# Attention with a spectral mix: in the full runs the value sums leave their PSUM bank after every run, and that bank also holds score tiles; scores and maxima over 64 rows

## The chip, the cores and the metric

The kernel runs on one core of a Trainium2 chip. The metric is the device time of one execution in microseconds (us). All matmuls are fp32 data: most are in the one-pass form (tiles of type F32R, split by the kernel into a high and a low part), the value products of the attention in the plain fp32 form.

## The reference

The kernel computes a gated mix of two layers over a sequence of 2048 rows of 512.

```python
g = _sigmoid((x * gate_w).sum(-1, keepdims=True))
a = _A_ref(x, dft_seq_re, dft_seq_im, dft_hid_re, dft_hid_im)   # y = Cr @ (x Hr^T) - Ci @ (x Hi^T)
b = _B_ref(x, wqkv, wo)                                          # softmax attention, 32 heads of 16
return g * a + (1 - g) * b
```

For each head the attention needs scores `q @ k^T / 4` (2048 x 2048), a softmax over them, and the product with the values (16 columns). The softmax here takes off each row's maximum, so the scores are worked out twice: once for the maxima, once for the exponentials.

## The kernel before

**Stages.** First come the projections of q and k, then those of v together with one half of the hidden transform, then a long middle part that runs the attention of all heads and, beside it, the sequence transform, and last the output projection. Heads are handled in pairs (`p`, 16 of them). A pair's q and k stand in `qs[p % 2]` and `ks[p % 2]`: head `h` of the pair has partitions 64h to 64h+47 (16 rows each of high times high, high times low, low times high). Rows 64h+48 and 64h+49 of `qs` take the negated row maxima (high and low part), the same rows of `ks` are ones, so that the scores come out of the matmul with the maximum already taken off. `load_stacks` loads a pair, `m_parts` and `m_rows` make the rows of maxima: VectorE reduces and transposes, GpSimd splits, and eight small DMAs write the rows, four of them issued by GpSimd for head 1 and the rest by SyncE.

**Three kinds of matmul share the tensor engine.** `a_tile` computes a 128 x 512 tile `a` of raw scores over 48 rows, and VectorE takes its maxima (`mx`). `scores` computes a 128 x 512 tile `s` over 50 rows, and ScalarE writes its exponentials to `pt`. `d` is a chain of 48 products, each in two halves of 64 rows, that accumulates one 128 x 512 tile of the sequence transform (class `Chain`, `dft`); its end is copied out by ScalarE (`y`). A `d` on one half of the array's rows and an `a` or `s` on the other half run at the same time. The fourth kind are the value products in `pv`: for each unit (`u`, a pair's block of 128 keys against 1024 queries) four matmuls with 17 columns of weights (16 values and a column of ones) and all 128 rows, each on its own strip of 32 columns of the array, accumulating in `acc`.

**Runs.** The order on every engine is written out by hand. The middle part is a sequence of runs (`segment`), each one following a pattern of slots. A slot issues one `d` and one `a` or `s`; `|` issues the value products of one unit. There are 26 runs of the thin patterns, then 192 of the pattern `FULL` (96 pairs of runs, the two halves of the same `d` operands), then 26 of the pattern `NINE`. A full run has 16 `d`, 8 `s`, 8 `a` and two units of value products. The digit behind a slot's letter is the PSUM bank of its tile. The first `d` of a run waits for the reader of the tile that the last slot of the run before made, and the last value product of a full run waits, by a dependency added by hand, for the run's last exponential (`exponential`).

**PSUM.** There are eight banks of 128 x 512 fp32: six (`six`, numbers 0 to 5) turn over among `s` and `a` tiles, one holds the tile `d`, and one holds `acc`. The sums of a pair's half of the queries accumulate in `acc` over 16 units (8 runs); then `acc` is copied to `oe` in SBUF (by VectorE in full runs, by ScalarE elsewhere) and two DMAs store it.

**GpSimd's queue.** GpSimd splits the chunks of the sequence transform's matrix into high and low parts (`c_split`: a cast and a subtraction for every 12 operands of `d`, each chunk needing its loaded `craw` and a pair of buffers that the `d` matmuls have finished with), makes the parts of the maxima, issues its four row DMAs, and does some multiplications of the normalisation (`no`, `nh`). All of this stands in one queue, in program order.

Of the kernel before, what the change touches and what calls it, by code (L numbers as in the profile page):

```python
# [31 lines left out]
def mix_kernel(ctx: ExitStack, tc: tile.TileContext, xa_t, xa, wqkv, w_hid, w_seq, wo, gate_w, out):  # L32
# [8 lines left out]
    six = [ctx.enter_context(tc.tile_pool(name=f"ps{i}", bufs=1, space=PSUM)) for i in range(6)]  # L41

    used = list(range(6))

    class Ring:
# [5 lines left out]
        def tile(self, shape, dtype, name, bank=None):  # L51
            i = min(self.banks, key=used.index) if bank is None else bank
            t = six[i].tile(shape, dtype, name=name, tag="t")
            self.touch(i)
            self.of[id(t)] = (t, i)
            return t
# [11 lines left out]
    psO = ctx.enter_context(tc.tile_pool(name="psO", bufs=1, space=PSUM))  # L68
# [6 lines left out]
    qk_d = [dram.tile([2, D, S], F32, name=f"qk{c}") for c in range(2)]  # L75
    b_d = [dram.tile([P, 2, D], F32, name=f"b{s}") for s in range(NT)]
# [21 lines left out]
    acc = psO.tile([P, 512], F32, name="acc")  # L98
# [179 lines left out]
    def a_tile(i, h, ps=None, bank=None):  # L278
# [4 lines left out]
        r = slice(64 * h, 64 * h + 48)  # L283
# [34 lines left out]
    nc.gpsimd.memset(ones, 1.0)  # L318
    nc.gpsimd.memset(vt[:, :, :, 16:17], 1.0)
    load_stacks(0)  # L320
    wos = [staged(wo[:, kt]) for kt in range(KT)]
    for i in range(2):
        for h in range(2):
            for tb in range(2):
                nc.sync.dma_start(ks[i][64 * h + 48:64 * h + 50, tb * 2 * D:(tb + 1) * 2 * D].bitcast(F32), ones)
# [433 lines left out]
    pts = {}  # L759

    def scores(u, qb, h, bank=(psS, "s"), number=None):
# [11 lines left out]
        rr = slice(64 * h, 64 * h + 50)  # L773
# [14 lines left out]
    def pv(u, full=False):  # L788
# [4 lines left out]
        pt = pts.pop(u)  # L793
        for j in range(4):
            h = j % 2
            i = nc.tensor.matmul(acc[32 * j:32 * j + 17], vt[:, kt, p, 16 * h:16 * h + 17], pt[:, j],  # L796
                                 start=kt == 0, stop=kt == NT - 1)
        if kt == NT - 1:
            oe = work.tile([P, 512], F32, name="oe", bufs=2)
            if full:  # L800

                nc.vector.tensor_copy(oe, acc)
            else:
                nc.scalar.copy(oe, acc)
            for qb in range(2):
                nc.sync.dma_start(o_d[hf][p, :, qb * 512:(qb + 1) * 512], oe[64 * qb:64 * qb + 64])
# [70 lines left out]
    FULL = "s2 a3 s4 a1 s5 s2 a0 s3 a4 s1 a5 s2 a0 s3 a4 a1 | |"  # L877
# [10 lines left out]

    streams = [stream(h) for h in range(2)]
# [11 lines left out]
    def values(full=False):  # L901
        nonlocal valued
        i = pv(valued, full)
# [3 lines left out]
    def segment(pattern, half, ds, stop):  # L907
# [5 lines left out]
        for n, slot in enumerate(pattern.split()):  # L913
# [3 lines left out]
            if slot == "|":  # L917
                i = values(pattern == FULL)
# [129 lines left out]
```

## Time and profile before

| | |
|---|---|
| time, median of 3 runs | 1698.53 us (1698.32 to 1698.54) |
| span of the profiled execution | 1696.8 us |
| granted TensorE clock, mean | 0.999 |
| instructions | 33721 |
| VectorE busy | 81% |
| ScalarE busy | 67% |
| GpSimd busy | 26% |

The profile is of one execution. Its span reaches from the first to the last instruction; the time of a run is a little longer. TensorE counts as busy whenever a matmul is in flight, and matmuls are pipelined, so that a busy TensorE may still be held up. In the rows of the profile PE is TensorE's matmuls, PEld its weight loads, DVE is VectorE, ACT ScalarE, POOL GpSimd and SP SyncE; L774 is line 774 of the kernel before, and a tile stands under its name in the program (`acc`, `s`, `a`, `d`, `pt`).

### The profile page before, as it was taken

To read this page: it belongs to the slowest core of one execution; us is meant where nothing else is said; L and a number is where in the kernel's file an instruction comes from. 1 tells how busy PE (TensorE), PEld (TensorE's weight loads), DVE (VectorE), ACT (ScalarE), POOL (GpSimd) and SP (SyncE) were. 2 spreads that over 40 slices of the span, in tenths; PEclk is the share of its full clock that TensorE was granted. 3 is DMA by queue.
4 is the path that set the end of the run, shared out by engine and by line. 5 is a ranking of instruction groups with operands and counts; after the bars stand their busy time and mean duration, and the time that the engine had idled before them with its cause. 6 is when DMAs were issued, how large, how long until landed. Compare 5 with 4: busy or idle time off the path is not lost.

```text
span 1696.8 us, 33721 instructions
## 1 busy us (share of the span) xinstructions
PE 1689.2 (100%) x13040; PEld 1076.1 (63%) x13040; DVE 1366.7 (81%) x2313; ACT 1138.6 (67%) x2242; POOL 449.6 (26%) x554
## 2 busy tenths in 40 slices
PE   9999999999999999999999999999999999999998
PEld 7888855556666666666666666666666666655544
DVE  5439888888888888888888888888888888889854
ACT  5212377777766777666777677776667776678886
POOL 0101122322222333222222343322323343211110
PEclk9999999999999999999999999999999999999999
DMA  8963600314141434314156435224141535362114
GB/s 294 344 146 132 161 8 13 47 39 76 57 76 46 88 98 97 73 39 82 38 95 243 96 108 109 68 63 77 50 83 58 120 111 101 129 187 39 36 30 138
DMA packets 82274, 165.10 MB, mean 97 GB/s; under 512 B 19460, under 2 KB 19954, under 8 KB 78274
## 3 DMA queue, kind: packets, MB, share of 16 engines
q1 hardware_dynamic: 77874, 161.99, 37.1%
q8 instruction: 103, 1.69, 0.4%
q0 software_dynamic: 3808, 0.30, 0.2%
q10 hardware_dynamic: 432, 0.66, 0.1%
q14 instruction: 57, 0.47, 0.1%
HBM read 107.73 MB, written 54.52 MB: 96 GB/s over the span
## 4 chain that ended last, share of the span: by engine, by line
PE 99%; DMA 0%; DVE 0%; DVEq 0%; ACT 0%; SPq 0%; issue 0%
PE d L451 33%; PE acc L796 27%; PE s L774 14%; PE a L284 12%; PE s L365 3%; PE s L397 1%; PE d L365 1%; PE acc L782 1%; PE a L106 1%; PE s L107 1%; PE a L107 1%; PE s L106 1%; PE s L105 1%; PE a L105 1%; PE s L451 1%; PE a L451 0%
## 5 line engine op out<-in xcount | busy, mean ns | idle before, releaser
L286 DVE TENSOR_REDUCE mx<-a 128x1 f32<-128x512 f32 x2026 | 1239.9, 681 | 213.1 <-PE a L284 199.1
L775 ACT ACTIVATE pt<-s 128x512 f32<-128x512 f32 x2006 | 1023.2, 620 | 403.0 <-PE s L774 390.5
L774 PE MATMUL s<-qs,ks 50*128 50x512 f32 x2006 | 794.0, 422 | 0.0
L284 PE MATMUL a<-ks,qs 48*128 48x512 f32 x2026 | 744.5, 398 | 0.0
L451 PE MATMUL d<-xab,ch 64*128 64x512 f32 x2016 | 647.8, 396 | 0.0
L774 PEld LDWEIGHTS s<-qs,ks 50*128 50x128 f32 x2006 | 365.4, 185 | 228.5 <-issue 177.5
L796 PE MATMUL acc<-pt,vt 128*17 128x512 f32 x3968 | 484.2, 596 | 0.0
L284 PEld LDWEIGHTS a<-ks,qs 48*128 48x128 f32 x2026 | 370.3, 186 | 53.2 <-DVE mx L286 23.2
L451 PE MATMUL d<-xab,cl 64*128 64x512 f32 x1008 | 399.4, 396 | 0.0
L451 PEld LDWEIGHTS d<-xab,ch 64*128 64x128 f32 x2016 | 366.7, 184 | 21.6
L435 POOL CAST ch<-craw 128x512 fp32r<-128x512 f32 x126 | 77.1, 612 | 549.1 <-PE a L284 282.2
L796 PEld LDWEIGHTS acc<-pt,vt 128*17 128x17 f32 x3968 | 102.3, 96 | 184.7 <-issue 184.5
L451 PEld LDWEIGHTS d<-xab,cl 64*128 64x128 f32 x1008 | 185.7, 184 | 10.5
L436 POOL TENSOR_TENSOR cl<-craw,ch 128x512 fp32r<-128x512 f32 x126 | 162.1, 1287 | 10.2
L309 POOL DMA_DIRECT2D qs<-mt x119 | 67.0, 568 | 150.3 <-DVE mt L303 147.8
L451 PE MATMUL d<-wre,xab 64*128 64x512 f32 x336 | 90.5, 402 | 0.0
L451 PEld LDWEIGHTS d<-wre,xab 64*128 64x128 f32 x336 | 59.0, 185 | 38.4 <-issue 23.3
L451 PE MATMUL d<-wo_hl,o_hl 64*128 64x512 f32 (+1 forms) x246 | 68.1, 409 | 0.0
L451 PEld LDWEIGHTS d<-wo_hl,o_hl 64*128 64x128 f32 (+1 forms) x246 | 42.3, 185 | 29.5 <-issue 12.1
L101 ACT CAST hl<-s 128x512 fp32r<-128x512 f32 x28 | 16.1, 587 | 58.5 <-PE s L365 31.4
L647 POOL TENSOR_TENSOR yp<-yp,few 128x512 f32<-128x512 f32 x12 | 15.4, 1283 | 112.4 <-ACT few L646 112.4
L469 POOL CAST xab<-y 128x512 fp32r<-128x512 f32 x16 | 9.8, 611 | 127.8 <-ACT y L467 99.6
(168 smaller groups left out, 1009.6 us busy)
## 6 DMA issues: line engine op xcount, KB each, us to landing
craw<-w_seq SPq DMA_DIRECT2D x128, 256.0 KB
qk<-hl SPq DMA_DIRECT2D x32, 512.0 KB
qs<-qk SPq DMA_DIRECT2D x96, 128.0 KB
ks<-qk SPq DMA_DIRECT2D x96, 128.0 KB
b<-hl SPq DMA_DIRECT2D x16, 512.0 KB
xab<-b SPq DMA_DIRECT2D x16, 512.0 KB
o<-oe SPq DMA_DIRECT2D x62, 128.0 KB
oh<-nh SPq DMA_DIRECT2D x12, 512.0 KB
```

Of the source, the lines that this page charges most:

```text
L105: nc.tensor.matmul(ps, sh, mh, start=first, stop=False)
L106: nc.tensor.matmul(ps, sh, ml, start=False, stop=False)
L284: nc.tensor.matmul(ps, qs[p % 2][r, qt * P:(qt + 1) * P], ks[p % 2][r, kb * 512:(kb + 1) * 512], start=True, stop=True)
L286: user = nc.vector.tensor_reduce(mx[p % 2][:, h, qt, kb:kb + 1], ps, AX.X, ALU.max)
L309: (nc.gpsimd if own else nc.sync).dma_start(rows.rearrange("v (q b c) -> v b q c", q=8, b=4)[:, b], mt[hf][32 * b + h:32 * b + 32:2])
L365: i = nc.tensor.matmul(ps, st[r], mv[r], start=not half and not j, stop=half == 1 and j == 11)
L435: nc.gpsimd.tensor_copy(h1, raw)
L436: nc.gpsimd.tensor_tensor(l1, raw, h1.bitcast(F32), ALU.subtract)
L451: i = nc.tensor.matmul(self.ps, st[r], mv[r], start=not self.begun, stop=stop)
L774: nc.tensor.matmul(ps, ks[p % 2][rr, kt * P:(kt + 1) * P], qs[p % 2][rr, q0:q0 + 512], start=True, stop=True)
L775: return nc.scalar.activation(pts[u][:, 2 * qb + h], ps, AF.Exp, bias=0.0, scale=DH ** -0.5)
L796: i = nc.tensor.matmul(acc[32 * j:32 * j + 17], vt[:, kt, p, 16 * h:16 * h + 17], pt[:, j], start=kt == 0, stop=kt == NT - 1)
```

## The change

In the full runs the sums no longer stay in `acc` for 8 runs. Each run starts a new `acc` tile with its first unit and closes it with its second; a new function `evacuate` copies it to SBUF with ScalarE: the first of the 8 into `total` (an `oe` buffer), the others into `few`, which GpSimd then adds to `total`. Behind the last one the two DMAs store `total`. The VectorE copy falls away. The first products of a full run use 32 columns of weights in place of 17, so that every row of the strip is written. The last thin run closes its partial sums in the same way, and the first run of the pattern `NINE` starts with a zeroed `acc`.

Between two uses by `acc`, its bank (now number 6) takes one `s` and one `a` tile of each full run, and the pattern `FULL` is another one: the order of `s` and `a` and all bank numbers differ.

`a_tile` and `scores` now work over 64 rows of each head. Rows 50 to 63 of `ks` and `qs` are zeros that are written once; rows 48 and 49 of `qs`, which hold the maxima of an earlier pair, are zeroed from a small DRAM tile `z_d` at each `load_stacks`, two more DMAs for a pair. At the start 18 more small DMAs write the zeros.

```diff
@@ load_stacks
         for h in range(2):
             rows = slice((2 * p + h) * DH, (2 * p + h + 1) * DH)
             o = 64 * h
+            if p > 1:
+                nc.sync.dma_start(q_t[o + 48:o + 50].bitcast(F32), z_d)
@@ a_tile
-        r = slice(64 * h, 64 * h + 48)
+        r = slice(64 * h, 64 * h + 64)
@@ setup
+    zeros = st1.tile([16, 2 * D], F32, name="hl", bufs=4)
+    nc.gpsimd.memset(zeros, 0.0)
...
-                nc.sync.dma_start(ks[i][64 * h + 48:64 * h + 50, tb * 2 * D:(tb + 1) * 2 * D].bitcast(F32), ones)
+                cols = slice(tb * 2 * D, (tb + 1) * 2 * D)
+                nc.sync.dma_start(ks[i][64 * h + 48:64 * h + 50, cols].bitcast(F32), ones)
+                nc.sync.dma_start(ks[i][64 * h + 50:64 * h + 64, cols].bitcast(F32), zeros[:14])
+                nc.sync.dma_start(qs[i][64 * h + 48:64 * h + 64, cols].bitcast(F32), zeros)
+    for tb in range(2):
+        nc.sync.dma_start(z_d[:, tb * 2 * D:(tb + 1) * 2 * D], zeros[:2])
@@ scores
-        rr = slice(64 * h, 64 * h + 50)
+        rr = slice(64 * h, 64 * h + 64)
@@ evacuate, pv
+    def evacuate(p, hf, done):
+        nonlocal total
+        if total is None:
+            total = work.tile([P, 512], F32, name="oe", bufs=2)
+            nc.scalar.copy(total, acc)
+        else:
+            nc.scalar.copy(few, acc)
+            nc.gpsimd.tensor_tensor(total, total, few, ALU.add)
+        if done:
+            for qb in range(2):
+                nc.sync.dma_start(o_d[hf][p, :, qb * 512:(qb + 1) * 512], total[64 * qb:64 * qb + 64])
+            total = None
+
-    def pv(u, full=False):
+    def pv(u, full=False, close=False):
...
+        begin, done = acc is None or kt == 0, kt == NT - 1
+        if acc is None:
+            acc = psO.tile([P, 512], F32, "acc")
+            if not full:
+                nc.vector.memset(acc, 0.0)
+        width = 32 if full and begin else 17
+        v = vt[:, kt].rearrange("p n d -> p (n d)")[:, 33 * p:]
         for j in range(4):
             h = j % 2
-            i = nc.tensor.matmul(acc[32 * j:32 * j + 17], vt[:, kt, p, 16 * h:16 * h + 17], pt[:, j],
-                                 start=kt == 0, stop=kt == NT - 1)
-        if kt == NT - 1:
-            oe = work.tile([P, 512], F32, name="oe", bufs=2)
-            if full:
-
-                nc.vector.tensor_copy(oe, acc)
-            else:
-                nc.scalar.copy(oe, acc)
...
+            i = nc.tensor.matmul(acc[32 * j:32 * j + width], v[:, 16 * h:16 * h + width], pt[:, j],
+                                 start=begin, stop=done or close)
+        if done or close:
+            evacuate(p, hf, done)
+            if close:
+                acc = None
         return i
@@ patterns
-    FULL = "s2 a3 s4 a1 s5 s2 a0 s3 a4 s1 a5 s2 a0 s3 a4 a1 | |"
+    FULL = "a5 s4 a2 s0 a3 s6 a5 s4 s1 s0 s2 a6 a3 a4 s5 a1 | |"
@@ segment
-                i = values(pattern == FULL)
-                if n == len(pattern.split()) - 1 and pattern == FULL:
+                end = n == len(pattern.split()) - 1
+                i = values(pattern == FULL, end and (pattern == FULL or valued == thin))
+                if end and pattern == FULL:
```

TensorE's order at the end of a full run and the start of the next, first of the kernel before, then of the changed one (a row is line, operation, output from inputs, weight columns by moving columns or the output's shape, and the engines whose semaphores it waits for):

```order
L451 MATMUL d<-xab_173,ch 128x512
L284 MATMUL a<-ks_941,qs_939 128x512 [waits DVE_49]
L451 MATMUL d<-xab_173,cl 128x512
L284 MATMUL a<-ks_941,qs_939 128x512 [waits Activation_49]
L796 MATMUL acc<-pt,vt 17x512 x7
L796 MATMUL acc<-pt,vt 17x512 [waits Activation_49]
```

```order
L785 MATMUL s<-qs_940,ks_942 128x512 [waits DVE_49]
L461 MATMUL d<-xab_174,cl 128x512
L287 MATMUL a<-ks_942,qs_940 128x512 [waits Activation_49]
L829 MATMUL acc<-pt,vt 32x512 [waits DVE_49]
L829 MATMUL acc<-pt,vt 32x512 x3
L829 MATMUL acc<-pt,vt 17x512 x3
L829 MATMUL acc<-pt,vt 17x512 [waits Activation_49]
L287 MATMUL a<-ks_942,qs_940 128x512
L461 MATMUL d<-xab_173,cl 128x512 [waits DVE_49]
```

The last score `s` of the run has moved from the third slot from the end to the last but one, the first value product has a wait on VectorE (for the maxima that were taken from the bank that `acc` now uses), and the next run begins with an `a`.

ScalarE's order over some full runs, before and after, where `nh` is the cast in the normalisation of a finished block of heads:

```order
L775 ACTIVATE pt<-s 128x512 x32
L101 CAST nh<-no 128x512
L775 ACTIVATE pt<-s 128x512 x16
L506 ACTIVATE y<-d,g 128x512
```

```order
L786 ACTIVATE pt<-s 128x512 x8
L806 COPY few<-acc 128x512
L102 CAST nh<-no 128x512
L786 ACTIVATE pt<-s 128x512 x8
L806 COPY few<-acc 128x512
```

Every eight exponentials are now followed by a copy of `acc`, and the cast stands behind that copy where it stood directly behind the exponentials.

GpSimd's order around four row DMAs in the changed kernel:

```order
L807 TENSOR_TENSOR oe<-oe,few 128x512 [waits Activation_49]
L301 CAST nhl_168<-nm_166 128x16 [waits DVE_49]
L302 TENSOR_TENSOR nhl_168<-nm_166,nhl_168 128x16 [waits Pool_49]
L807 TENSOR_TENSOR oe<-oe,few 128x512 [waits Activation_49]
L312 DMA qs_941<-mt_170 2x8x32 [waits DMASW7_49,DVE_49]
L312 DMA qs_941<-mt_170 2x8x32 [waits DMASW0_49]
L312 DMA qs_941<-mt_170 2x8x32 [waits DMASW1_49]
L312 DMA qs_941<-mt_170 2x8x32 [waits DMASW2_49]
L445 CAST ch<-craw 128x512 [waits DMAHW7_49,PE_49]
```

An addition of `few` to the totals (an `oe` buffer) now stands ahead of the parts of the maxima and ahead of the four row DMAs.

More of the change, by code (lines that the diff above doesn't have):

```diff
@@ L39, in mix_kernel @@
     ctx.enter_context(tc.manual_schedule())
-    six = [ctx.enter_context(tc.tile_pool(name=f"ps{i}", bufs=1, space=PSUM)) for i in range(6)]
-    used = list(range(6))
+    seven = [ctx.enter_context(tc.tile_pool(name=f"ps{i}", bufs=1, space=PSUM)) for i in range(7)]
+    used = list(range(7))
     class Ring:
@@ L75, in mix_kernel @@
     qk_d = [dram.tile([2, D, S], F32, name=f"qk{c}") for c in range(2)]
+    z_d = dram.tile([2, S], F32, name="z")
     b_d = [dram.tile([P, 2, D], F32, name=f"b{s}") for s in range(NT)]
```

15 lines of the change are left out of this document (8 added, 7 removed).

## The prediction

> **What bounds the kernel now.** I read the page first (busy shares, the chain that ended last), then the timeline of one full run in the middle, then the waits.
>
> ```profile
> PE 1689.2 (100%) x13040; PEld 1076.1 (63%) x13040; DVE 1366.7 (81%) x2313; ACT 1138.6 (67%) x2242; POOL 449.6 (26%) x554
> PE 99%; DMA 0%; DVE 0%; DVEq 0%; ACT 0%; SPq 0%; issue 0%
> L796 PE MATMUL acc<-pt,vt x3096: 592/592/607, 354.9 to 1494.4; 128*17 128x512 f32 x194
> ```
>
> TensorE is in flight all the time and the chain is TensorE to 99%. The third row (the value products between 355 and 1496 us) says where: a run has 16 such records, so 3096 of them are 193.5 runs' worth, the 192 full runs and a little. They fill two thirds of the span, and what one of them costs decides. One full run:
>
> ```profile
> 804.85 0.50 PE L774 MATMUL s<-qs,ks 50*128 50x512 f32 x1
> 805.19 0.39 PE L284 MATMUL a<-ks,qs 48*128 48x512 f32 x1
> 805.39 4.03 ACT L775 ACTIVATE pt<-s 128x512 f32<-128x512 f32 x8 [1.87 <-PE s L774]
> 805.62 4.87 DVE L286 TENSOR_REDUCE mx<-a 128x1 f32<-128x512 f32 x8 [1.02 <-PE a L284]
> ...
> 806.04 0.18 PEld L774 LDWEIGHTS s<-qs,ks 50*128 50x128 f32 x1
> ...
> 807.31 0.39 PE L284 MATMUL a<-ks,qs 48*128 48x512 f32 x1
> ...
> 807.51 0.18 PEld L774 LDWEIGHTS s<-qs,ks 50*128 50x128 f32 x1
> 807.54 0.47 PE L774 MATMUL s<-qs,ks 50*128 50x512 f32 x1
> 807.85 0.40 PE L284 MATMUL a<-ks,qs 48*128 48x512 f32 x1
> ...
> 808.43 0.39 PE L451 MATMUL d<-xab,cl 64*128 64x512 f32 x1
> 808.58 0.40 PE L284 MATMUL a<-ks,qs 48*128 48x512 f32 x1
> 808.91 1.91 PE L796 MATMUL acc<-pt,vt 128*17 128x512 f32 x16
> 809.35 0.21 PEld L796 LDWEIGHTS acc<-pt,vt 128*17 128x17 f32 x4 [0.31 <-issue]
> 809.78 0.12 PEld L796 LDWEIGHTS acc<-pt,vt 128*17 128x17 f32 x4 [0.22 <-issue]
> 810.75 0.50 PE L774 MATMUL s<-qs,ks 50*128 50x512 f32 x1
> 811.29 0.60 ACT L775 ACTIVATE pt<-s 128x512 f32<-128x512 f32 x1 [1.87 <-PE s L774]
> ```
>
> Times within a run count from its first matmul from here on. The period is 810.75 - 804.85 = 5.90 us. Four things are to be seen. (1) The last `d` starts at 3.58 and the last `a` at 3.73: the stream of `s` and `a` ends 0.15 late, and the value products start 0.33 behind it, at 4.06. (2) Part of that is a wait for a bank. Exponentials end every (4.03 - 0.60) / 7 = 0.49 us, so the fourth ends at 805.39 + 0.60 + 1.47 = 807.46; the weights of the `s` that takes the same bank (slot 11) load at 807.51, its matmul takes 0.47 in place of 0.39, and the next `a` starts 0.31 later, where the nine steps before it took (807.31 - 805.19) / 9 = 0.235. (3) The value products last 810.75 - 808.91 = 1.84. Their last one waits by hand for the eighth exponential: that ends at 809.42, and the waiting weights load at 809.35 + 0.21 - 0.10 = 809.46. They are needed at 809.78, so this wait is free now, by 0.3. (4) ScalarE is idle 1.87 and VectorE 1.02 between runs.
>
> **The change, part by part.** *Banks.* With seven banks and the new slots no tile meets a busy bank. Exponentials end at 1.37 + 0.49k and maxima every 4.87 / 8 = 0.61; the nearest meeting is the `a` of slot 15, whose bank is released at 1.37 + 4 x 0.49 = 3.33 and wanted at 3.6. That takes the 0.08 of the stall away. The bank that `acc` takes over is read by VectorE last: the tile of slot 11 starts at 0.34 + 10 x 0.235 = 2.69, its maxima begin 0.43 later (805.19 to 805.62) and are done by 3.12 + 0.68 = 3.80, against value products at 3.9. Free by 0.1.
>
> *64 rows.* The matmul of 48 rows takes 398 ns, that of 64 rows where both halves run 64 rows takes 392; the weight loads do not differ.
>
> ```profile
> L284 PE MATMUL a<-ks,qs 48*128 48x512 f32 x2026 | 744.5, 398 | 0.0
> L365 PE MATMUL s<-wch,xab 64*128 64x512 f32 x186 | 39.5, 392 | 0.0
> L284 PEld LDWEIGHTS a<-ks,qs 48*128 48x128 f32 x2026 | 370.3, 186 | 53.2 <-DVE mx L286 23.2
> L796 PEld LDWEIGHTS acc<-pt,vt 128*17 128x17 f32 x3968 | 102.3, 96 | 184.7 <-issue 184.5
> ```
>
> Up to 6 ns a slot; I take 3, so that over 14 steps the stream ends 0.04 earlier, its last tile starting at 0.34 + 14 x 0.232 = 3.59, level with `d`. The Trainium skill, page "TensorE: Matmul & The Clock Gate", section "LDWEIGHTS (loading the stationary operand)", says that a load's time goes by its columns and not by its rows. The load rows here agree (186 ns for 48 rows); by that alone the term for 64 rows would be nil, but the matmul rows differ.
>
> *TensorE's own period* is then 3.59 + 0.33 + 1.84, and 0.01 for the loads with 32 columns: 5.77 to 5.78.
>
> *ScalarE's period.* The run now starts with an `a`; the first `s` is in slot 1 and starts at 0.34, its exponential at 0.34 + 0.43 = 0.77, and the eight end at 0.77 + 0.60 + 7 x 0.49 = 4.80, where they ended at 4.57. The copy of `acc` stands ahead of them:
>
> ```profile
> 292.07 1.05 PE L796 MATMUL acc<-pt,vt 128*17 128x512 f32 x8
> 293.19 0.59 ACT L804 COPY oe<-acc 128x512 f32<-128x512 f32 x1
> 293.67 1.09 ACT L775 ACTIVATE pt<-s 128x512 f32<-128x512 f32 x2
> ```
>
> It starts 0.07 behind the products' end, takes 0.59, and an exponential behind it ends 0.49 later. In a full run the products end at 0.07 of the next one (808.91 + 1.91 against 810.75), so the copy lies from 0.14 to 0.73 and allows the first exponential to end at 1.22; it ends at 1.37 anyway. The copy hides in the 1.87 us of idle time; without that cover it would cost 0.49. But the exponential that the last value product waits for is 0.23 later and the products are 0.14 earlier: the load fires at 4.85, and the matmuls of that unit are due at 3.92 + 0.87 = 4.80. So this hand-made wait is what ends last. From the load the run needs the exposed part of the load and then 0.95 (809.78 to 810.75, less the 0.02 by which the fourth strip follows the first). Exposed are between 0.01 (the first pass after a fresh load lasts 809.35 - 808.91 = 0.44, a later one 0.43) and the 0.096 of a whole load. I take 0.01, since that row is the same operation. Period 4.85 + 0.01 + 0.95 = 5.81 to 5.82; with the load exposed, 5.90. The larger of the two periods counts: **5.82, 0.08 less than now; 192 x 0.08 = 15.4 us.** VectorE doesn't bind: its last maxima end at 3.12 + 4 x 0.61 = 5.56, before the first `d` of the next run is due.
>
> *The cast behind the copy.* Twelve full runs have the `nh` cast.
>
> ```profile
> 1013.44 2.58 ACT L775 ACTIVATE pt<-s 128x512 f32<-128x512 f32 x5
> 1015.82 0.69 ACT L101 CAST nh<-no 128x512 fp32r<-128x512 f32 x1
> ```
>
> It ended 0.49 behind the exponentials, in the idle time (1016.51 against 1016.02). Now it stands behind the copy, ends at 0.73 + 0.49 = 1.22, and the first exponential ends at 1.71 in place of 1.37: 0.34 on ScalarE's period, **+4 us** in 12 runs.
>
> *GpSimd* gets 168 additions (192 less one in eight) of the kind of the first row below, 1.28 us each, 13% of its time. They hide in its idle time. What they push back is the four row DMAs behind them:
>
> ```profile
> L647 POOL TENSOR_TENSOR yp<-yp,few 128x512 f32<-128x512 f32 x12 | 15.4, 1283 | 112.4 <-ACT few L646 112.4
> 799.15 2.24 POOL L309 DMA_DIRECT2D qs<-mt  x4 [5.66 <-DVE mt L303]
> qs<-mt POOLq DMA_DIRECT2D x119, 2.0 KB, 1.7
> POOL ch L435 <- DMA craw<-w_seq: 41.6, 5, 12.7
> ```
>
> They began 0.1 to 0.2 into a run; now they wait for copy and addition, until 0.73 + 0.05 + 1.28 = 2.06, some 1.9 later. The fourth was issued at about 800.8 and landed at 802.5; its reader is the `s` loaded at 806.04 in the run after. Of 3.5 us slack 1.5 are left: nothing on the path, unless GpSimd is behind. It is behind where it waits for `craw` (fourth row, five times); such a wait now also holds an addition and so the next copy. I put +1 us for it, between 0 and 20.
>
> *The other runs.* In the 52 thin and `NINE` runs of about 14 slots, 64 rows may save up to 52 x 14 x 0.006 = 4.4 us, or nothing where another engine holds them. I take -2. *The start:*
>
> ```profile
> 100.14 0.42 SPq L271 DMA_DIRECT2D qs<-qk  x1
> 109.59 7.61 SPq L325 DMA_DIRECT2D ks<-hl  x8
> 128.06 0.62 ACT L101 CAST hl<-raw 128x512 fp32r<-128x512 f32 x1
> ```
>
> 26 small DMAs stand where 8 took 7.61. At 0.42 each SyncE is through by 121, at 0.95 by 134; the cast at 128.06 reuses the buffer of the ones and may wait up to 4 us. I put +1 (0 to 3). The DMAs of `z_d` lie a whole pair ahead of their readers: nothing.
>
> **Sum** against the profiled span of 1696.8: -15.4 + 4 + 1 - 2 + 1 = -11.4, so 1685.4. The median of the runs is 1.7 above that span: **1687 us.** Its own range is 1680 to 1694.
>
> **Rivals.** *The waiting load is exposed* (0.096): ScalarE's loop then runs at 5.90, the runs gain nothing, the cast's 4 and the ones above remain: 1703, between no change and slower. For it: no row shows a load that comes late within the value products. Against: the 0.44 against 0.43. *TensorE's period holds*: the fourth strip, alone at the end, makes up the 0.04. Then 192 x 0.125 = 24 and 3.5 for the casts: 1698.5 - 24 + 3.5 = 1678. *GpSimd's queue* (the slower side): the rows of maxima, or the buffer `few`, come late because a chunk split or a wait for `craw` stands ahead of the addition. It decides from the point where GpSimd is over 1.5 us behind at such a run; a split is 0.61 + 1.29. If 24 of these runs lose 0.8 each, that is 19 us: 1706. Against it: GpSimd is busy 26% and its splits have two chunks of slack. *The late load waits for the other strips*: if it cannot run while their matmuls are in flight, it waits out a pass of 0.43 from 4.80: 5.23 + 0.01 + 0.95 = 6.19, 0.37 over 5.82, or 71 us: 1758. Against it the loads at 809.35 to 809.56, which fire with 16 products in flight from 808.91. The Trainium skill, same page, section "Part 3: Packing small matmuls — row/col tiling", states that loads overlap with matmuls in flight only where the row group differs, which would give this rival; the trace disagrees at those rows.
>
> **Numbers.** Forecast 0.52, exposed load 0.17, TensorE's period 0.16, GpSimd 0.12, strips 0.03. A measurement of this kernel can tell 0.2%, 3.4 us, from no change. Faster: nearly all of the first and all of the third, a little of the others, 0.67; same: half of the exposed load, a few of the rest, 0.13; slower 0.20. The range 1676 to 1706 holds the forecast, the third case and most of the second, and leaves out about 0.18.
>
> **What would show it.** Right: a period of about 5.82 in full runs, the `s` and `a` streams ending within 0.05 of `d`, no matmul over 0.45 in mid-run, the last load of the value products 0.9 behind their start in place of 0.55, exponentials ending at 4.8, runs with the cast 0.3 longer, four row DMAs about 2 us later and no reader waiting for them. Wrong: a period of 5.90 or more with the last load's matmul 0.1 behind its load; TensorE waiting on row DMAs; a copy to `few` waiting for GpSimd; or an engine other than ScalarE behind the last wait.

## The result and the profile after

| | before | after |
|---|---|---|
| time, median of 17 runs each | 1698.54 us (1698.01 to 1699.00) | 1699.56 us (1696.09 to 1704.69) |
| ratio, 95% interval | | 1.0011 (1.0003 to 1.0019) |
| span of the profiled execution | 1696.8 us | 1699.1 us |
| full run, median period | 5.902 us | 5.830 us |

The change gains nothing: its median lies 0.1% above that of the kernel before, 1.0 us, while its own runs differ by 8.6. The full runs did get shorter, nearly as forecast, and 192 of them are worth some 14 us. The same time is lost elsewhere. First the page of the kernel after: its busy shares, its chain, and two groups that are new (line, engine, operation, count | busy us, mean ns | idle before it, and what ended most of that).

```profile
PE 1683.4 (99%) x13040; PEld 1024.1 (60%) x13040; DVE 1371.5 (81%) x2290; ACT 1250.0 (74%) x2435; POOL 661.6 (39%) x724
PE 95%; DMA 3%; POOL 1%; issue 0%; SPq 0%; DVE 0%; ACT 0%; DVEq 0%; POOLq 0%
L807 POOL TENSOR_TENSOR oe<-oe,few 128x512 f32<-128x512 f32 x169 | 218.4, 1293 | 489.8 <-ACT few L806 481.4
L806 ACT COPY few<-acc 128x512 f32<-128x512 f32 x169 | 99.1, 586 | 189.4 <-PE acc L829 178.2
```

TensorE is still in flight nearly all the time, but its share of the chain fell from 99% to 95%: DMAs and GpSimd, to which the page before gives nothing, now have 4%. GpSimd went from 26% to 39% busy. Now one full run, in the timeline (start, duration, both in us, then the instructions and the idle time before them):

```profile
831.15 2.00 PE L829 MATMUL acc<-pt,vt 128*32 128x512 f32 x16
831.61 0.11 PEld L829 LDWEIGHTS acc<-pt,vt 128*17 128x17 f32 x3 [0.30 <-issue]
832.04 0.19 PEld L829 LDWEIGHTS acc<-pt,vt 128*17 128x17 f32 x5 [0.32 <-issue]
833.08 0.49 PE L287 MATMUL a<-ks,qs 64*128 64x512 f32 x1
833.25 0.59 ACT L806 COPY few<-acc 128x512 f32<-128x512 f32 x1 [1.18 <-PE acc L829]
833.62 5.04 DVE L289 TENSOR_REDUCE mx<-a 128x1 f32<-128x512 f32 x8 [0.76 <-PE a L287]
833.86 4.03 ACT L786 ACTIVATE pt<-s 128x512 f32<-128x512 f32 x8
833.91 1.29 POOL L807 TENSOR_TENSOR oe<-oe,few 128x512 f32<-128x512 f32 x1 [4.51 <-ACT few L806]
...
836.62 0.39 PE L461 MATMUL d<-xab,ch 64*128 64x512 f32 x1
836.66 0.39 PE L287 MATMUL a<-ks,qs 64*128 64x512 f32 x1
836.98 1.99 PE L829 MATMUL acc<-pt,vt 128*32 128x512 f32 x16
```

From one run's value products to the next, 836.98 - 831.15 = 5.83. The last `a` starts 0.04 behind the last `d`, where it was 0.15: the stall at a busy bank is gone. In the third row the last of five loads starts at 832.04 + 0.19 - 0.10 = 832.13, 0.98 behind the first product. The load just ahead of it is the one that waits by hand for the eighth exponential; it fires 0.97 behind the first product (here and in the median over the full runs; before, 0.55). The exponentials of the run that begins at 833.08 end at 833.86 + 4.03 = 837.89, 4.81 behind its first matmul. The copy and the addition lie beside this work. So a normal run went as the prediction drew it. The whole span, stage by stage, from the PE timeline of the two profiled executions:

| stretch | before | after | difference |
|---|---|---|---|
| start, to the first value products | 205.66 | 209.44 | +3.78 |
| thin runs, to the first full run's products | 154.68 | 154.19 | -0.49 |
| first to last full run's products | 1127.51 | 1122.87 | -4.64 |
| from there to the last value products | 196.43 | 200.01 | +3.58 |
| tail, to the end of the span | 12.5 | 12.6 | +0.07 |

The third row is made of 191 x (5.830 - 5.902) = -13.75; +3.4 in the twelve runs with the `nh` cast (6.11 us each); +5.64 in three runs of 7.32, 7.12 and 8.69 us; and 0.07 of the rest. So 13.75 was gained in the full runs, 0.49 in the thin ones, and 16.4 lost again: 3.8 at the start, 3.6 at the end, 5.6 in three runs, 3.4 in twelve.

**The start.** PE's timeline of the kernel after, then the windows view of before and of after (window | us, and busy us of PE, PEld, DVE, ACT and POOL, then the granted clock, the DMA share and GB/s):

```profile
118.64 0.39 PE L287 MATMUL a<-ks,qs 64*128 64x512 f32 x1
121.52 0.76 PE L287 MATMUL a<-ks,qs 64*128 64x512 f32 x1 [2.49 <-DMA qs<-hl]
```

```profile
118.00:128.00 10.00, 10.00 (x90) 8.20 (x88) 7.72 (x14) 1.39 (x4) 1.29 (x1) 1.00 0.28 95
```

```profile
118.00:128.00 10.00, 7.51 (x53) 6.12 (x51) 3.96 (x6) 0.00 (x0) 0.00 (x0) 0.83 0.36 58
```

The second maxima tile reads 64 rows and waits 2.49 us for the zeros (their buffer is called `hl`). Behind the wait a matmul takes 0.76 in place of 0.39, and the granted clock over these 10 us is 0.83: for 3.4 us it was a half.

**The end of the full runs.** The first run of `NINE` starts with a zeroed `acc`. VectorE's timeline of after, then PE's:

```profile
1488.97 3.08 DVE L289 TENSOR_REDUCE mx<-a 128x1 f32<-128x512 f32 x5 [0.79 <-PE a L287]
1492.16 0.48 DVE L824 MEMSET acc<- 128x512 f32 x1
```

```profile
1492.80 1.24 PE L829 MATMUL acc<-pt,vt 128*17 128x512 f32 x8 [1.98 <-DVE acc L824]
1495.54 1.72 PE L829 MATMUL acc<-pt,vt 128*17 128x512 f32 x8
```

The zeroing stands behind five maxima in VectorE's queue; TensorE waits 1.98 for it, and again the clock halves: the granted clock is a half from 1493.53 to 1496.94, and the eight products of the second row take 1.72, where such eight take 1.05 at full clock (so at 1488.07 with the cast on VectorE, below).

**A late row of maxima.** The chain that ended last, around the run at 902 (start, duration, what):

```profile
892.17 1.28 POOL oe L807
893.45 0.95 POOL qs L312 x2
...
894.52 0.55 POOL qs L312
895.07 5.23 DMA qs<-mt
900.31 0.25 issue
900.55 0.46 PE s L785
```

The addition delays the row DMAs: GpSimd issues its four from 893.40 on, while SyncE issues the other four from 891.25. The four take 1.7, 4.0, 4.7 and 5.2 us to land, in their order (the median of all is 1.7), and an `s` waits for the last (1.03 us in PE's timeline). Four loads of `xab`, 512 KB each, were issued between 894.02 and 895.85: the first row DMA went out ahead of them, the second with the first of them, the other two among them.

**A late addition.** GpSimd's timeline around 975, then ScalarE's:

```profile
973.08 0.61 POOL L445 CAST ch<-craw 128x512 fp32r<-128x512 f32 x1 [6.99 <-DMA craw<-w_seq]
973.77 1.27 POOL L446 TENSOR_TENSOR cl<-craw,ch 128x512 fp32r<-128x512 f32 x1
975.00 1.28 POOL L807 TENSOR_TENSOR oe<-oe,few 128x512 f32<-128x512 f32 x1
```

```profile
976.32 0.58 ACT L806 COPY few<-acc 128x512 f32<-128x512 f32 x1 [2.60 <-POOL oe L807]
```

The chunk split waits 6.99 us for its load, the addition stands behind it, and the next copy cannot write `few` until the addition has read it. The copy holds the bank of `acc`, and the bank's next user is the score of slot 6 (`s6`). At 1353.56 the same copy waits 4.17 (there the split had waited 5.21 for TensorE). TensorE's waits in the kernel after show all four losses (who waited for what: us in total, times, longest):

```profile
PE s L785 <- ACT few L806: 2.7, 2, 2.1
PE a L287 <- DMA qs<-hl: 2.5, 1, 2.5
PE acc L829 <- DVE acc L824: 2.0, 1, 2.0
...
PE s L785 <- DMA qs<-mt: 1.0, 1, 1.0
```

### The profile page after: what moved, and what is told of

Same layout as the page of the kernel before. It is cut to its first block, busy times and chain, and to the rows that moved or that the text cites. A ratio compares the mean times of both kernels' runs of the same rounds, so it can differ in the third digit from the quotient of the medians.

```text
span 1699.1 us, 34567 instructions
## 1 busy us (share of the span) xinstructions
PE 1683.4 (99%) x13040; PEld 1024.1 (60%) x13040; DVE 1371.5 (81%) x2290; ACT 1250.0 (74%) x2435; POOL 661.6 (39%) x724
## 4 chain that ended last, share of the span: by engine, by line
PE 95%; DMA 3%; POOL 1%; issue 0%; SPq 0%; DVE 0%; ACT 0%; DVEq 0%; POOLq 0%
PE acc L829 28%; PE d L461 25%; PE a L287 17%; PE s L785 15%; PE s L375 3%; PE d L375 1%; PE acc L793 1%; DMA ks<-qk 1%; PE a L108 1%; PE a L106 1%; PE s L108 1%; PE s L106 1%; PE a L107 1%; PE s L107 1%; DMA raw<-wo 1%; PE s L461 1%
## 5 line engine op out<-in xcount | busy, mean ns | idle before, releaser
L289 DVE TENSOR_REDUCE mx<-a 128x1 f32<-128x512 f32 x2026 | 1258.8, 684 | 220.3 <-PE a L287 186.7
L287 PE MATMUL a<-ks,qs 64*128 64x512 f32 x2026 | 729.8, 405 | 2.5 <-DMA qs<-hl 2.5
L785 PE MATMUL s<-qs,ks 64*128 64x512 f32 x2006 | 692.8, 402 | 3.7 <-ACT few L806 2.7
L829 PE MATMUL acc<-pt,vt 128*17 128x512 f32 (+1 forms) x3968 | 502.1, 600 | 2.0 <-DVE acc L824 2.0
L287 PEld LDWEIGHTS a<-ks,qs 64*128 64x128 f32 x2026 | 367.5, 184 | 224.5 <-issue 165.5
L807 POOL TENSOR_TENSOR oe<-oe,few 128x512 f32<-128x512 f32 x169 | 218.4, 1293 | 489.8 <-ACT few L806 481.4
L785 PEld LDWEIGHTS s<-qs,ks 64*128 64x128 f32 x2006 | 363.1, 184 | 65.3 <-issue 18.4
L806 ACT COPY few<-acc 128x512 f32<-128x512 f32 x169 | 99.1, 586 | 189.4 <-PE acc L829 178.2
L829 PEld LDWEIGHTS acc<-pt,vt 128*17 128x17 f32 (+1 forms) x3968 | 103.6, 101 | 217.6 <-issue 155.7
```

The source lines that it names most:

```text
L287: nc.tensor.matmul(ps, qs[p % 2][r, qt * P:(qt + 1) * P], ks[p % 2][r, kb * 512:(kb + 1) * 512], start=True, stop=True)
L289: user = nc.vector.tensor_reduce(mx[p % 2][:, h, qt, kb:kb + 1], ps, AX.X, ALU.max)
L785: nc.tensor.matmul(ps, ks[p % 2][rr, kt * P:(kt + 1) * P], qs[p % 2][rr, q0:q0 + 512], start=True, stop=True)
L806: nc.scalar.copy(few, acc)
L807: nc.gpsimd.tensor_tensor(total, total, few, ALU.add)
L829: i = nc.tensor.matmul(acc[32 * j:32 * j + width], v[:, 16 * h:16 * h + width], pt[:, j], start=begin, stop=done or close)
```

## The experiments

All were timed in five rounds beside the kernel before, whose median was 1698.7 to 1698.8 in each. The kernel after was not timed again with them, and with its spread a difference from its 1699.56 holds to about 1 us (an estimate from the 17 runs). The profile of each is one execution, and the three long runs differ in size from one execution to the next, so a profile shows where time goes and the median what it is worth.

**Four losses, one at a time.** *Fewer rows for the first maxima*, so that they read no zeros:

```diff
-        r = slice(64 * h, 64 * h + 64)
+        r = slice(64 * h, 64 * h + (64 if p else 48))
```

> The changed kernel with the maxima of the first pair of heads over 48 rows again (the other pairs stay at 64), so that the first tiles of maxima no longer read the zeros that are written at the start. Theory: the changed kernel loses 3.8 us at the start, 2.5 of them a wait for the DMAs of the zeros at 119 us and 1.3 of them the half clock that follows it; without the wait the first value products start at 205.7 us as in the kernel before (209.4 in the changed one), the clock is not halved at 121 us, and the time falls by 3.8 to about 1696. Rival: the wait only moves on to the next reader behind those DMAs (the casts and loads that stand behind them in SyncE's queue), and the first value products stay later than 208.

1697.37 us, ratio 0.9996 (0.9987 to 1.0005): 2.2 under the changed kernel, where 3.8 were expected. First value products at 206.76, not at 205.7. The wait at 121 and the half clock are gone; 1.1 us stay, and ScalarE's timeline says where:

```profile
130.04 0.62 ACT L102 CAST hl<-raw 128x512 fp32r<-128x512 f32 x1 [1.70 <-DMA ks<-hl]
```

This cast takes over the buffer of the ones and waits for their DMAs, which now stand among 16 more. That is the wait the prediction had named; it is the smaller of the two.

*No zeroing*: the first products into a fresh `acc` are 32 columns wide in `NINE` too.

```diff
-        width = 32 if full and begin else 17
+        width = 32 if fresh else 17
...
-            if not full:
-                nc.vector.memset(acc, 0.0)
```

> The changed kernel without the zeroing of the value sums' bank by VectorE at the first run behind the full ones: that run's first products use 32 columns of weights instead, as the full runs do. Theory: the zeroing stands behind five maxima in VectorE's queue, TensorE waits 2.1 us for it and then runs at half clock for 3.4 us; without it the stretch from the last full run's value products to the last value products of the kernel falls from 200.0 us to about 196.4, as before the change, and the time by 3.6 to about 1696. Rival: the lag is the new wait for the copy and the addition at this place, and 200 stays.

1696.97 us, 0.9989 (0.9980 to 0.9998). The end stretch is 196.43, that of the kernel before to the hundredth. So the whole +3.58 hung on this instruction, the half clock behind its wait included.

*Two buffers in turn for `few`*:

```diff
+    few2 = [few, work.tile([P, 2, D], F32, name="few2", tag="w15")[:, 0]]
...
-            nc.scalar.copy(few, acc)
-            nc.gpsimd.tensor_tensor(total, total, few, ALU.add)
+            few2.reverse()
+            nc.scalar.copy(few2[0], acc)
+            nc.gpsimd.tensor_tensor(total, total, few2[0], ALU.add)
```

> The changed kernel with two buffers in turn for the sums that GpSimd adds. Nothing else moves; GpSimd stays as late as it is. Theory: two of the three long full runs (7.1 and 8.7 us in the profile of the changed kernel, against 5.83) are ScalarE's copy waiting for the one buffer, held by an addition that stands behind a cast waiting for its load; with two buffers these runs go, about 4 us in that execution, and the spread over executions (1696 to 1705) narrows to under 4 us; the run of 7.3 us that waits for row DMAs may stay. Rival: the copies then run ahead but the row DMAs, or the chunk splits, are what is late, and the long runs stay, of another cause.

1696.74 us, 0.9987 (0.9978 to 0.9995). The long runs at 979 and 1357 are gone, the one at 904 stays (8.09 us): two of the three hang on the buffer, the third on the row DMAs. The runs spread over 4.5 us, where the theory said under 4.

*The `nh` cast on VectorE*:

```diff
-            hi_lo(hl[:, 0], hl[:, 1], t[:, 0], nc.gpsimd)
+            nc.vector.tensor_copy(hl[:, 0], t[:, 0])
+            nc.gpsimd.tensor_tensor(hl[:, 1], t[:, 0], hl[:, 0].bitcast(F32), ALU.subtract)
```

> The changed kernel with the twelve casts of the normalised heads on VectorE in place of ScalarE. Theory: these casts stand behind the copy on ScalarE and make twelve full runs 6.11 us long in place of 5.83; on VectorE they lie in its idle time between runs, the twelve runs go back to about 5.83 and 3.4 us are saved. Rival: VectorE is as tight there as ScalarE, its first maxima come 0.4 or more later, a bank is then late, and the runs stay over 6.0.

1694.66 us, 0.9974 (0.9965 to 0.9984): 4.9 under the changed kernel, where 3.4 were expected. The cast takes VectorE 0.41 us, and the twelve runs of 6.11 are back at 5.83; only four runs are over 5.95 now, the row DMAs' and `few`'s. The end stretch was 198.55 in this profile with the zeroing still there: TensorE again waits 1.98 for it, but no half clock follows, and the stretch is 2.1 over before. So of the 3.58 about 1.5 was the clock.

**What ends last in a full run.** *The hand-made wait taken out* (the matmul still waits for its own operands; it is the extra dependency that goes):

```diff
-                if end and pattern == FULL:
-
-                    tc.add_manual_dep(i.ins, exponential.ins.name,
-                                      mybir.DependencyInfo(mybir.DependencyClass.Sync, mybir.DependencyReason.DATA))
```

> The changed kernel without the dependency added by hand of a full run's last value product on its last exponential. Theory: in the changed kernel this wait ends last in every full run (its weights load 0.95 us behind the first value product, and the products take 1.39 from the first start to the last start where 1.32 is the least), so the period falls from 5.83 to TensorE's own, about 5.76, 192 x 0.07 = 13 us less, and the last load fires 0.45 to 0.55 behind the first product. Rival: the period stays at 5.83, because the next run's first tile then waits for the same exponential, or because TensorE's own slots take that long.

1686.58 us, 0.9927 (0.9914 to 0.9941). PE's timeline, the first and the last of a stretch of full runs of the kernel after, then of this one:

```profile
398.52 2.01 PE L829 MATMUL acc<-pt,vt 128*32 128x512 f32 x16
...
755.41 2.02 PE L829 MATMUL acc<-pt,vt 128*32 128x512 f32 x16
```

```profile
402.11 1.92 PE L829 MATMUL acc<-pt,vt 128*32 128x512 f32 x16
...
754.33 1.92 PE L829 MATMUL acc<-pt,vt 128*32 128x512 f32 x16
```

61 runs lie between the rows of each, four of them with the cast. Less 0.28 and 0.32 for each cast, the periods are (356.89 - 1.1) / 61 = 5.83 and (352.22 - 1.3) / 61 = 5.75. So the wait cost 0.08 of each run, 14.6 us in 192; the median fell by 13.0. Before the change it cost nothing, as the next run shows.

*The same wait taken out of the kernel before*:

```diff
-                if n == len(pattern.split()) - 1 and pattern == FULL:
-                    tc.add_manual_dep(i.ins, exponential.ins.name,
...
```

> The kernel before without the dependency of a full run's last value product on its last exponential. Theory: there it has 0.3 us to spare, the weights load 0.55 behind the first product and are needed at 0.87, so nothing changes: period 5.90, time 1698.5, within 0.1%. Rival: the wait costs something in the kernel before too, and a part of the 13 us is to be had without the change.

1698.70 us, 1.0000 (0.9991 to 1.0009), period 5.903. The wait became the end of the run because the change moved both of its sides: the run now begins with an `a`, so that its exponentials end 4.81 behind its first matmul where they ended at 4.57, and the value products begin at 836.98 - 833.08 = 3.90 where they began at 4.06.

**What the 64 rows do.** *The kernel after with 48 and 50 rows and no zeros*:

```diff
-        r = slice(64 * h, 64 * h + 64)
+        r = slice(64 * h, 64 * h + 48)
...
-        rr = slice(64 * h, 64 * h + 64)
+        rr = slice(64 * h, 64 * h + 50)
```

> The changed kernel with scores over 50 and maxima over 48 rows again and without any of the zeros; banks, pattern and copies stay changed. Theory: ScalarE's chain sets the period, so the rows do not matter in the full runs: 5.82 to 5.84 stays, and the time falls by the 3.8 us of the start, to about 1696. Rival: the 64 rows carry part of the gain: the stream of s and a then ends 0.06 to 0.1 later in every run, and the period goes to 5.88 or more, which is 10 us and makes the kernel slower than 1700.

1696.14 us, 0.9985 (0.9976 to 0.9994). The period is 5.828, the same, but for nine runs behind a cast, which take 5.94; the first value products come at 205.75, as before the change. With 48 rows the last `a` starts 3.61 behind the run's first matmul, with 64 rows 3.58 (medians), and the hand-made wait covers the difference. Here the rows gain next to nothing and the zeros cost the start.

*The kernel before with 64 rows and the zeros* (only that part of the change):

```diff
-        r = slice(64 * h, 64 * h + 48)
+        r = slice(64 * h, 64 * h + 64)
...
+                nc.sync.dma_start(ks[i][64 * h + 50:64 * h + 64, cols].bitcast(F32), zeros[:14])
+                nc.sync.dma_start(qs[i][64 * h + 48:64 * h + 64, cols].bitcast(F32), zeros)
...
-        rr = slice(64 * h, 64 * h + 50)
+        rr = slice(64 * h, 64 * h + 64)
```

> The kernel before with the 64 rows and the zeros alone. Theory: in the kernel before the stream of s and a ends last in a full run, 0.15 behind d; 64 rows save 3 ns a slot or 0.04 a run, 8 us in all, and the start costs 3.8: about 1694. Rival 1: rows cost and save nothing in the runs, the start alone counts: 1702. Rival 2: the whole of 6 ns a slot and more shows, 0.1 a run: 1683.

1702.11 us, 1.0022 (1.0013 to 1.0031). Start 209.08, period 5.902: the start's loss in full, and no gain, against my theory of 0.04 a run. In the kernel before the wait for the bank takes up what the rows give: the second to the fifth step from one `s` or `a` to the next take 0.232 in place of 0.237, and still the last `a` starts 3.72 behind the run's first matmul in both (medians over the full runs).

**Together.** *All five edits* (the four above, and no hand-made wait; the lines that stand for each):

```diff
+        r = slice(64 * h, 64 * h + (64 if p else 48))
...
+            few2.reverse()
...
+        width = 32 if fresh else 17
...
+            nc.vector.tensor_copy(hl[:, 0], t[:, 0])
...
-                    tc.add_manual_dep(i.ins, exponential.ins.name,
```

> The changed kernel with all five edits: maxima of the first pair over 48 rows, no zeroing at the first run behind the full ones, two buffers for the sums, the casts on VectorE, and no hand-made wait. Theory: the costs add up, 3.8 + 3.6 + about 4 + 3.4 + 13 = 28 us under the changed kernel: about 1672. Rival: the edits share a bound, the period of the full runs stays near 5.83 with TensorE waiting on another engine, and only the start and the end are saved: about 1688.

1673.79 us, 0.9854 (0.9840 to 0.9867). The period is 5.755 and the end stretch 196.46. Besides one full run of 6.27, two losses are left in its profile: the start (207.36; the cast of the ones' buffer waits 2.00), and one run of 7.52 at 893, where PE's timeline has an `s` waiting for a row:

```profile
890.70 0.47 PE L787 MATMUL s<-qs,ks 64*128 64x512 f32 x1 [1.31 <-DMA qs<-mt]
```

*The ones' DMAs ahead of the zeros'*, on top of that:

```diff
+    for t in (ones, zeros):
...
+                    if t is ones:
+                        nc.sync.dma_start(ks[i][64 * h + 48:64 * h + 50, cols].bitcast(F32), ones)
+                        continue
```

> e8_all with the eight DMAs of the ones issued ahead of all DMAs of the zeros. Theory: what is left of the loss at the start in e8_all (first value products at 207.4 us against 205.7 before the change) is a cast of ScalarE at about 130 us that reuses the buffer of the ones and waits for the last of their DMAs, which stands behind 14 DMAs of zeros; with the ones first it goes, the first value products start at 205.7 and the time is 1.7 lower, 1672. Rival: the zeros' own DMAs hold the next users of the queue as long, and 207 stays.

1673.75 us, 0.9852 (0.9838 to 0.9865). The first value products come at 205.57, so the start's loss is gone, yet the median hardly moves. In the profiled execution the run at 893 took 9.86 us: the `s` waited 2.59 for its row, with a half clock behind it.

```profile
890.31 0.47 PE L790 MATMUL s<-qs,ks 64*128 64x512 f32 x1 [2.59 <-DMA qs<-mt]
```

Here the last row DMA took 6.7 us to land. Whether the executions that were not profiled lose their time at the same place is not shown.

*The additions behind the row DMAs*: GpSimd's part of `evacuate` is held back and recorded at the run's end.

```diff
-            nc.gpsimd.tensor_tensor(total, total, few2[0], ALU.add)
+            held.append(partial(add_late, p, hf, done, total, few2[0]))
...
+        run_late()
```

> e9_ones_first with GpSimd's additions (and the stores behind them) recorded at the end of a run, behind the row DMAs and the parts of the maxima instead of ahead of them. Theory: the one long full run left in e8_all (7.5 us at about 893) is TensorE waiting for a row DMA that GpSimd issues 2 us later than in the kernel before, behind the addition, at a place where 512 KB loads slow its landing; with the rows ahead of the addition that run is under 6.1 and the time 1 to 1.7 under e9. Rival: the landing behind the large loads is late by itself and the run stays at 7 or more.

**1669.97 us (1669.76 to 1670.31), 0.9831 (0.9818 to 0.9844): this version beats both kernels.** GpSimd's timeline at the same place:

```profile
879.25 2.25 POOL L312 DMA_DIRECT2D qs<-mt  x4 [3.83 <-DVE mt L306]
881.51 1.30 POOL L828 TENSOR_TENSOR oe<-oe,few 128x512 f32<-128x512 f32 x1
```

The row DMAs go out as soon as VectorE has made the rows, all four ahead of the first `xab` load (issued at 881.78); each lands in 1.7 us, and no run near 890 is long. So the order in the queue was the cause, and the rival (late by itself) is refuted. The time is 3.8 under the version before it, more than the 1 to 1.7 expected. One run of 6.29 is left in the whole profile, and the four runs of this kernel lie within 0.55 us, where the 17 of the change as made spread over 8.6.

*The best version with 48 and 50 rows*:

```diff
-        r = slice(64 * h, 64 * h + (64 if p else 48))
+        r = slice(64 * h, 64 * h + 48)
...
-                    nc.sync.dma_start(ks[i][64 * h + 50:64 * h + 64, cols].bitcast(F32), zeros[:14])
-                    nc.sync.dma_start(qs[i][64 * h + 48:64 * h + 64, cols].bitcast(F32), zeros)
...
-        rr = slice(64 * h, 64 * h + 64)
+        rr = slice(64 * h, 64 * h + 50)
```

> e10_rows_ahead with scores over 50 and maxima over 48 rows and no zeros anywhere. Here TensorE's own slots set the period of a full run, so this shows what the rows are worth. Theory from e6 and e7 (rows save nothing): period as in e10, about 5.755, time within 2 us of e10. Rival, the prediction's: 3 to 6 ns a slot, so a period of 5.80 or more and a time 8 us or more above e10.

1677.04 us, 0.9871 (0.9856 to 0.9886). PE's timeline of the best version, then of this one:

```profile
399.44 1.92 PE L848 MATMUL acc<-pt,vt 128*32 128x512 f32 x16
...
756.46 1.92 PE L848 MATMUL acc<-pt,vt 128*32 128x512 f32 x16
```

```profile
400.94 1.92 PE L837 MATMUL acc<-pt,vt 128*32 128x512 f32 x16
...
754.13 1.93 PE L837 MATMUL acc<-pt,vt 128*32 128x512 f32 x16
```

357.02 / 62 = 5.758 against 353.19 / 61 = 5.790. Where TensorE's own slots bind, 64 rows are worth 0.03 a run, against the theory of nothing and a little under the rival's 5.80. The median moves by 7.1 us. Of the 7.6 between the two profiled spans 6.3 lie in the full runs; another 1.2 lie at the start (first value products at 206.19 against 204.97), for a reason that stays open.

## Why the prediction was right or wrong

It said 1687, 11.5 us faster. The time is 1699.56: inside the range of 1676 to 1706, outside the forecast's own 1680 to 1694, and with no gain. On spans the sum was -11.4 and the profile shows +2.3, so 13.7 us are to be found. What failed is the price of all that the change adds beside the regular full run: the zeroed `acc` (put at nothing, cost 3.58), GpSimd's queue (put at 1, cost 5.64) and the start (put at 1, cost 3.78). Together they were put at 2 us and cost 13.0.

- **The full run, -15.4: right in mechanism and nearly in size** (-13.75). Forecast 5.82, measured 5.830. The hand-made wait ends last, as the step said, and without it the period is 5.754, a little below the 5.77 to 5.78 given for TensorE alone. The exposed part of the late load is small, as taken: with 0.096 the period would have been 5.90. This rival and the one that TensorE's own period holds are refuted for the kernel as made.
- **The strips: refuted.** The late load fires 0.97 behind the first product, while products of the other strips are in flight, and the period is 5.83, not 6.19. The rule of the Trainium skill that speaks for the rival ("TensorE: Matmul & The Clock Gate", "Part 3: Packing small matmuls — row/col tiling": loads overlap only where the row group differs) does not hold here, with all 128 rows in both.
- **The cast, +4: right** (+3.4, 0.283 a run against 0.34); with the cast on VectorE these runs return to 5.83.
- **The start, +1 (0 to 3): wrong.** It cost 3.78, above the upper bound. The step looked for the first reader of the small DMAs at the cast at 128.06, and so missed the maxima from 118.64 on, which read the rows of zeros as soon as they work over 64 rows. The edit to `a_tile` gave those DMAs a new, earlier reader, whose wait goes when the first pair is back at 48 rows. About 1.3 of it is the half clock behind the wait.
- **The end, not in the sum: the step that failed outright.** Nothing was priced for the zeroed `acc`. It is one instruction of 0.48 us, and it cost 3.58 in the profile (about 2.1 by TensorE's wait, 1.5 by the half clock behind it), because it stands behind five maxima in VectorE's queue and its reader is on the path. Without the instruction the end stretch is that of the kernel before.
- **GpSimd's queue, +1 (0 to 20): mis-sized**, 5.64. The mechanism was named, with both of its outlets (the row DMAs and `few`), and each of them was undone by an edit of its own. It happens three times, not 24, but for 1.3, 1.5 and 2.9 us and not 0.8. The slack of 1.5 us for the rows was worked out with a landing time of 1.7; here one took 5.23.
- **The other runs, -2: mostly wrong.** -0.49 in the thin runs; with the zeroing taken out the end stretch is just what it was before, so `NINE` gained nothing.
- **64 rows, 0.04 a run: right in size, wrong in place.** It shows only where TensorE's slots bind (0.03 with no hand-made wait); in the changed kernel the hand-made wait covers it, in the kernel before the bank does.

The errors of the terms, in the order of the sum, are 1.65 (runs), -0.6 (cast), 4.6 (GpSimd), 1.5 (other runs), 2.8 (start) and 3.6 (zeroing), with 0.15 of the rest: 13.7. All but one have the same sign. The largest, GpSimd's, sits in three full runs that differ from the rest; the next two are the end of the full runs and the start of the kernel. In all three what was added was not followed down to its first reader.

The wait that the forecast named as last was worth more than the forecast's whole gain: taking it out gives 13 us. The range held the time, but that was luck: it reached up to 1706 for 24 late runs of 0.8 each, of which three came, and for an exposed load, which did not. The 0.13 for "same" rested mostly on the exposed load, and what made the time the same was something else.

## What to carry to other kernels

When a change shortens the repeated part, price the edges with the same care: for every instruction that it adds at a stage's start or end, name the first reader and what stands ahead of it in its queue, because a 0.48 us instruction cost 3.6 us here, the half clock included. A wait that was added by hand for an old order of slots should be tried without when the order changes; it was free before and cost 0.08 a run after. And when an engine with slack gets work, put that work behind what others wait for (the row DMAs) and give its input a second buffer: both together took out the three long runs.

## What was not expected of the hardware

**A short wait of TensorE can halve its clock for 3.4 us, and need not.** Waits of 2.49 (at 121.52) and 1.98 (at 1492.80) were each followed by one such stretch; with the hand-made wait taken out, the same place at the start waited 2.21 and the clock stayed at 1.00 (windows view of that kernel, columns as above):

```profile
118.00:128.00 10.00, 7.79 (x69) 7.24 (x67) 5.39 (x9) 0.80 (x3) 0.00 (x0) 1.00 0.36 58
```

The first value products came at 209.44 in the one and 207.78 in the other. What decides is where the wait falls. In every profiled execution here the granted clock changes only at whole steps of 3.41 us, counted from the trace's first clock record. The windows view by these steps, two of the kernel after and two without the hand-made wait:

```profile
117.96:121.37 3.41, 1.07 (x9) 0.56 (x5) 0.69 (x1) 0.00 (x0) 0.00 (x0) 1.00 0.25 42
121.37:124.78 3.41, 3.26 (x16) 2.83 (x18) 0.69 (x1) 0.00 (x0) 0.00 (x0) 0.50 0.46 75
```

```profile
117.01:120.43 3.42, 2.25 (x19) 1.50 (x17) 0.69 (x1) 0.00 (x0) 0.00 (x0) 1.00 0.25 44
120.43:123.84 3.41, 2.36 (x21) 2.36 (x23) 1.13 (x2) 0.00 (x0) 0.00 (x0) 1.00 0.36 58
```

In the first pair the wait lies almost wholly inside one step: TensorE is busy 1.07 of 3.41 us, and the step behind it runs at 0.50. In the second the wait is divided over two steps (busy 2.25 and 2.36), and the clock stays. The wait of 1.98 for the zeroing went the same way: inside one step (busy 1.43) in the kernel after, divided over two (2.67 and 2.17) with the cast on VectorE, where the clock stayed. Over the profiled executions of all kernels here, from the first clock record (at 4 to 7 us) to the tail, ten steps had TensorE idle for 55% or more, and a half clock followed each; no step idle for 45% or less had one behind it. So an edit that moves the same wait by a microsecond can gain or lose some 1.5 us.

The Trainium skill, "TensorE: Matmul & The Clock Gate", section "What's actually happening", has a window of 4096 cycles, 3413 ns, that runs free of the kernel, and the length of the stretch agrees; that it takes an idle window of that length to slow the clock does not agree with waits of 2.0 and 2.5 us.

Such stretches, and long runs that differ in size, are the likely reason that the changed kernel spreads over 8.6 us and the kernel before over 1.0. The granted clock of each execution bears out the first: its mean is 0.999 in four runs of 1696.1 to 1699.4 us and 0.996 in four of 1701.2 to 1704.7, and one stretch takes 0.001 off it (half of 3.41 in 1699). Which waits they followed in the executions that were not profiled is not shown.

**A row DMA of 2 KB took 5.23 us to land,** three times its median, among four loads of 512 KB. Of the four row DMAs of that group the one issued 0.6 us ahead of the first load landed in 1.7, and in the best version all four, issued ahead of the loads, did.

**The score and maxima matmuls are cheaper over 64 rows than over 50 and 48** where both halves of the array work, by 0.032 us in a run of 16 slots (2 ns each), while their weight loads take the same 184 to 186 ns. Why is not settled.
